# Zero stores in a later slot, one group of products behind a matmul group, other PSUM banks for two small tiles

## Chip, cores and metric

One core of a Trainium2 chip runs the whole kernel. The metric is the device time of one execution in microseconds (us); the kernel before has a median of 1085.94 us over three runs.

## The reference

Three stages follow each other. A linear attention runs over 768 tokens of 4 batches and 8 heads of 40 channels; per token the state decays by `w`, loses a rank-one correction, and gains one:

```python
for t in range(S):
    y[:, :, t] = einsum('bhd,bhde->bhe', r[t], state)
    Sa = einsum('bhde,bhe->bhd', state, a[t])
    state = state * w[t] - einsum('bhd,bhe->bhde', Sa, b[t])
    state = state + einsum('bhd,bhe->bhde', v[t], k[t])
```

Its output, as 3072 rows of 320, goes through a gated product `x = (x @ w_a * (x @ w_b)) @ w_out` with an inner width of 1536. Last comes a layer of 8 experts: each row goes to the expert with the largest gate logit, `max(x @ w1[e], 0) @ w2[e]` with an inner width of 1024, scaled by the gate weight.

## The kernel before

**Attention and up projection (`phase1`).** The 768 tokens are cut into 12 chunks of 64. The recurrence inside a chunk is solved as matmuls with a triangular inverse, so a chunk needs: its decay products (`gp`, from `w`), score matrices per batch, the inverse of a 64 x 64 triangle, and a forward pass that carries the state. The loop `for c in range(NCH + 1)` has 24 slots `i` per step, and the dictionary `STEADY` (line 378) says which piece runs in which slot. Pieces of several chunks stand in one step: the forward pass of chunk c, scores and inverse for c+1 and c+2, loads for c+3.

Four engines (TensorE, VectorE, ScalarE, GpSimd) run their instructions in the order in which the program is written (`manual_schedule`). SyncE, which issues most transfers, is not among them; its queue is ordered by the scheduler. An engine stops at an instruction whose data or buffer is not there, and all that is written behind it on that engine waits too.

What matters around the change, by slot:

- Slot 5, for 2 <= c < 10: one store of zeros `zt` to the DRAM buffer `xs` (line 351), eight stores of 805 KB each. A memset of `zt` on GpSimd (line 498) stands two slots earlier. Expert rows are scattered into `xs` much later.
- Slot 5: `relayout` (line 690) reads the decay products out of the buffer of `w` into `gp`. Slot 7: `load_w` (line 534) loads `w` of a later chunk, 366 KB, into the one buffer `w`. Slots 11, 12, 13 and 15: `spans` (line 557), four checks of the range of `w` on ScalarE; their result is used only at the end of the kernel.
- Slots 7 and 19: `uv` loads (line 798). Slots 9 and 20: `vn` loads on ScalarE's queue (line 792). Slots 10 and 1: `r`. Slot 15 and 0: `bk` (line 540). Slots 18 and 20: `at` (line 589).
- Slots 7, 8, 15, 19: scores (lines 631 to 641); one slot after a pair is done its part `nd` is sent to DRAM (line 648), and `tinv` (lines 700 to 745) loads it back as `m` and a unit matrix as `xt`, builds the inverse of 32 x 32 blocks on VectorE (lines 716 and 722, two instructions for each of 31 rows) and sends it through DRAM into `s`.
- `t21a` (line 747) in slot 22 for batch pair 0 and in slot 26, which is slot 2 of the next step, for pair 1: two transposes on VectorE (line 755, `t`), 32 products of 32 x 32 on TensorE (line 759, `ta`, two PSUM banks) and two evictions on ScalarE (line 766, `pt`). `t21b` (lines 778 and 782, `tb`) follows two slots later and completes the triangle. The forward pass `forward` (lines 827 to 850, `px` and `pu`, evicted into `vn` and `xs`) stands in every second slot.
- Odd slots from 3 on: two up-projection groups from the list `units` (lines 338 to 341). A group is eight matmuls into one PSUM bank (line 1115, `pm`), evicted on ScalarE for `w_a` (line 1118, `ua`) and multiplied on VectorE for `w_b` (line 1127, `uh`), and stored every second time (line 1129, `hT`).

PSUM is cut in two pools: five banks under the tag `pa` (`psA`) for attention, down products and the like, three under `pm` (`psM`) for the groups.

**Down projection and gate (`MoeDown.run`).** It multiplies `hT` by `w_out` (line 1268, `py`), computes gate and expert number, counts slots (line 1303, `pr`, a tile of `psM`) and scatters each row to `xs` by indirect DMA on GpSimd (line 1321).

**Experts (`Experts.run`).** A list of jobs: (0, 0, 256) is the first 256 rows of expert 0, (0, 256, 384) the next 384, then the other experts. A job gathers its rows from `xs` (line 1515, `x`), transposes them on TensorE (line 1540), runs `up` (line 1562, `u`, eight tiles in `psM`, each read by ScalarE at line 1564 as `hh` and by VectorE at line 1565 as `hl`) and `down` (line 1582). The last counts and scatters of the gate stand inside job 0's `up`. In job 1's `up`, after the sixth tile, `said` (line 1607) adds up the verdict of all range checks: the product `pb` of the operand `bb` with ones, in `psM`.

Of the kernel before, what the change touches and what calls it, by code (L numbers as in the profile page):

```python
# [8 lines left out]
F32 = mybir.dt.float32  # L9
# [30 lines left out]
def kernel_body(tc, I, out, stage="full", dbg=None):  # L40
    nc = tc.nc
    ctx = ExitStack()
    with ctx:
# [36 lines left out]
        with ExitStack() as moe:  # L80
            with tc.manual_schedule(engines={E.PE, E.DVE, E.Activation, E.Pool}):
                down = None if stage == "up" else MoeDown(tc, I, moe, psA, psM, ident, hT, wo, xs)
                phase1(tc, I, cst, drm, psA, psM, ident, hT, mk_ident, wo, xs, span, tiny, down)
                if stage == "up":
                    return
                experts = Experts(tc, I, moe, psA, psM, ident, xs, out)
                down.run(experts, span, tiny, flag)
# [45 lines left out]
def phase1(tc, I, cst, drm, psA, psM, ident, hT, mk_ident, wo, xs, span, tiny, down):  # L133
    nc = tc.nc
# [3 lines left out]
    A = Attention(tc, I, att, mid, cst, drm, psA, ident, dv, ot, span)  # L138
# [46 lines left out]
    tinv = A.tinv(0)  # L185
# [16 lines left out]
    t1 = A.tinv(1, (uh, view(xt)))  # L202
# [8 lines left out]
    mix(t1[:lead], [lambda: A.forward((0, 0))] + conv.take(n3))  # L211
    t1 = t1[lead:]
    over = [A.spans(0, [t[:120, 0:L // 2].bitcast(F32) for t in sp])]
    units, tinv = [], t1
    for c in range(NCH + 1):
        T = dict(STEADY)
        if c == 0:
# [8 lines left out]
        for i in range(24):  # L226
# [41 lines left out]
                    A.t21b(c1, pr)  # L268
            if 1 <= c < NCH:
                for pr in on("t21a", i + 24):  # L270
                    A.t21a(c, pr)
                for pr in on("t21b", i + 24):
                    A.t21b(c, pr)
            for m in range(3):
# [63 lines left out]
            if i % 2 and (i >= T["group"] or len(units) > 24):  # L338
                for g in units[:2]:
                    g()  # L340
                units = units[2:]
            more = []
            if c < 2:
# [14 lines left out]
            n = T["tinv"][i]  # L358
            mix(tinv[:n], dv.take() + more)
            tinv = tinv[n:]  # L360
            if i == T["inverse"] and c2 < NCH:
                assert not tinv
                tinv = A.tinv(c2)
# [22 lines left out]

    "t21a": [22, 26], "t21b": [24, 28],
    "tinv": [0, 0, 2, 3, 5, 5, 2, 2, 5, 5, 5, 5, 5, 5, 5, 5, 3, 0, 0, 0, 0, 0, 0, 0],
    "group": 2, "fill": 5, "dsg": 2, "dxf": 0, "dtake": 3, "dh": 1, "dst": 3,
}  # L390
LAST = {"open": 21, "free": 6, "w": [1, 11], "load": [18, 20, 22], "gate": 14, "conv": [21, 22]}

# [72 lines left out]
def urow(b, o):  # L465
    return slice(C * (b % 2) + o, C * (b % 2) + o + R)


class Attention:
# [274 lines left out]
            out.append(lambda s=s, box=box: sub(s, box))  # L744
        return out

    def t21a(self, c, pr):

        nc = self.nc
        st = self.st[c]  # L750
        bs = 2 * pr, 2 * pr + 1
        s1 = [st["s1"][pr][:, x] for x in range(2)]
        t11 = self.p2.tile([128, 8, R], F32, tag="t11", name=f"t11_{c}_{pr}", bufs=1)
        for b in bs:
            nc.vector.transpose(out=t11[urow(b, 0)], in_=s1[b % 2][urow(b, 0), :, 0:R])  # L755
        pa = [self.ps.tile([128, 512], F32, tag="pa", name=f"ta{c}_{b}") for b in bs]
        for h in range(H):
            for b in bs:
                nc.tensor.matmul(  # L759
                    pa[b % 2][urow(b, R), R * h:R * h + R], s1[b % 2][urow(b, 0), h, R:C], t11[urow(b, 0), h, :],  # L760
                    start=True, stop=True)
        p = self.p2.tile([128, 8, R], F32, tag="pt", name=f"pt{c}_{pr}", bufs=1)
        st["p", pr] = p
        for b in bs:
            q = urow(b, R)
            nc.scalar.mul(p[q], pa[b % 2][q, :8 * R].rearrange("p (h t) -> p h t", t=R), -1.0)
# [653 lines left out]
class Experts:  # L1420
# [128 lines left out]
    def up(self, j, n, xt, then):  # L1549
        nc, p2 = self.nc, self.p2  # L1550
        x, ids, xh, xl = xt
        h1, l1 = self.w1[JOBS[j][0]]
        hs = []
        for f in range(FF2 // 128):
            fs = slice(128 * f, 128 * f + 128)
            p = self.psM.tile([128, 512], F32, tag="pm", name=f"u{j}_{f}")[:, 0:n]
            seq = [(h1[:, k, fs], xl[:, k]) for k in range(2)]
            seq += [(l1[:, k, fs], xh[:, k]) for k in range(2)]
            seq += [(h1[:, 2, fs], xl[:, 2]), (h1[:, 2, fs], xh[:, 2])]
            seq += [(h1[:, k, fs], xh[:, k]) for k in range(2)]  # L1560
            for i, (l, r) in enumerate(seq):
                nc.tensor.matmul(p, l, r, start=(i == 0), stop=(i == len(seq) - 1))
            hh, hl = (p2.tile([128, 512], F32R, tag=t, name=f"{t}{j}_{f}", bufs=12)[:, 0:n] for t in ("hh", "hl"))
            nc.scalar.activation(out=hh, in_=p, func=AF.Relu)  # L1564
            nc.vector.scalar_tensor_tensor(  # L1565
                out=hl, in0=p, scalar=0.0, in1=hh.bitcast(F32), op0=ALU.max, op1=ALU.subtract)
            hs.append((hh, hl))
            for g in then.get(f, ()):
                g()
        return hs  # L1570
# [21 lines left out]
    def verdict(self, ones, span, tiny, over, flag):  # L1592

        nc, p1 = self.nc, self.pw
        bb = p1.tile([128, 6], BF16, name="bb", bufs=1)
        nc.vector.memset(bb, 0.0)
        sp = p1.tile([120, 4], F32, name="sp", bufs=1)
        nc.vector.tensor_reduce(out=sp, in_=span, op=ALU.add, axis=AX.X)
        nc.vector.tensor_scalar(bb[0:120, 0:4], sp, 0.0, 0.0, op0=ALU.is_le, op1=ALU.is_equal)
        nc.vector.tensor_copy(bb[:, 4:5], over)  # L1600
        cn = p1.tile([128, 1], F32, name="cn", bufs=1)
        nc.vector.tensor_reduce(out=cn, in_=tiny[:, 0:NTINY], op=ALU.add, axis=AX.X)
        nc.vector.tensor_scalar(bb[:, 5:6], cn, 0.0, 0.0, op0=ALU.is_le, op1=ALU.is_equal)

        def said():
            pb = self.psM.tile([128, 6], F32, tag="pm", name="pb")
            nc.tensor.matmul(pb, ones, bb, start=True, stop=True)
            nc.vector.tensor_reduce(out=cn, in_=pb, op=ALU.max, axis=AX.X)
            nc.vector.tensor_scalar(flag, cn, 0.0, None, op0=ALU.is_gt)

        self.said = said

    def run(self, hooks):
        self.p2 = self.ctx.enter_context(self.tc.tile_pool(name="e2", bufs=2))
        s1 = lambda e: [lambda k=k: self.split1(e, k) for k in range(3)] if e < NE else []
        s2 = lambda e: [lambda k=k: self.split2(e, k) for k in range(4)] if e < NE else []
        for j, (e, off, n) in enumerate(JOBS):
            up, down = {}, {}
            put = lambda d, at, f: d.setdefault(at, []).append(f)
            if j == 0:  # L1620
                for at, f in hooks.items():
                    put(up, at, f)
            elif j == 1:
                put(up, 2, self.late)
                put(up, 5, lambda: self.said())
                for k, f in enumerate(s1(1) + [lambda: self.load1(2)] + s2(1) + [lambda: self.load2(2)]):
                    put(up, min(1 + k, 7), f)
                for k, f in enumerate(s1(2)):
                    put(down, min(k, 2), f)
            else:  # L1630
                for k, f in enumerate(s2(e + 1)):
                    put(up, 2 + k, f)
                for k, f in enumerate(s1(e + 2)):
                    put(down, min(k, 2), f)
# [265 lines left out]
```

## Time and profile before

| | us |
|---|---|
| runs | 1087.28, 1081.84, 1085.94 |
| median | 1085.94 |
| the profiled execution | 1086.37 |
| its span in the trace | 1084.6 |
| busy in it: TensorE matmul | 961.4 |
| VectorE | 705.0 |
| ScalarE | 572.8 |
| GpSimd | 391.6 |

The span runs from the first to the last instruction of the profiled execution. Names in rows are `out<-in` by the program's tile names; L759 is line 759 of the kernel before. PE is TensorE's matmul, DVE VectorE, ACT ScalarE, POOL GpSimd, SPq the queue of SyncE. A bracket at the end of a timeline row gives the idle time of the engine ahead of the row and what ended it. PEclk is TensorE's granted clock as a share of full speed.

### The profile page before, as it was taken

How to read it: one execution, taken by the hardware profiler on the slowest of the kernel's cores; microseconds unless marked ns; L12 is line 12 of the kernel's file. 1: busy time of each engine (PE TensorE's matmuls, PEld its weight loads, DVE VectorE, ACT ScalarE, POOL GpSimd, SP SyncE). 2: the span in 40 equal slices, each digit the busy share in tenths (PEclk: the TensorE clock that was granted, in tenths of full speed). 3: DMA queues.
4: the chain of work that ended last, by engine and by line, in shares of the span. 5: the costliest groups of instructions: out<-in, count | busy, mean ns of one | idle time of the engine just before them, and what ended most of it. 6: DMA issues, size and time to landing. Idle time of an engine off the chain costs nothing. (4 is left out here: it accounts for less than half of the span.)

```text
span 1084.6 us, 28183 instructions
## 1 busy us (share of the span) xinstructions
PE 961.4 (89%) x10879; PEld 909.3 (84%) x10879; DVE 705.0 (65%) x1891; ACT 572.8 (53%) x1365; POOL 391.6 (36%) x433
## 2 busy tenths in 40 slices
PE   4145389899999999999999999999999999999994
PEld 3045378899999899999999999899999889999994
DVE  8699589797978879797986832356568542222330
ACT  5357777666666566666665443433344354444530
POOL 4326544424232323234232112002226277666641
PEclk9655669999999999999999999999999999999998
DMA  8563454677686858678684233665665454444500
GB/s 206 143 179 82 113 132 106 158 142 172 162 191 165 178 153 165 156 157 173 154 197 119 60 91 108 186 187 162 184 200 173 160 168 146 133 150 144 160 16 17
DMA packets 218667, 158.59 MB, mean 146 GB/s; under 512 B 125269, under 2 KB 200630, under 8 KB 218524
## 3 DMA queue, kind: packets, MB, share of 16 engines
q1 hardware_dynamic: 205196, 137.33, 50.5%
q0 software_dynamic: 9808, 15.76, 4.8%
q10 hardware_dynamic: 3520, 3.61, 1.2%
q8 instruction: 88, 1.44, 0.6%
q14 instruction: 55, 0.45, 0.1%
HBM read 108.08 MB, written 44.60 MB: 141 GB/s over the span
## 5 line engine op out<-in xcount | busy, mean ns | idle before, releaser
L716 DVE TENSOR_TENSOR tmp<-m,xt 128x126 f32<-128x126 f32 (+22 forms) x372 | 117.6, 316 | 50.9 <-DMA xt<-in_one 34.9
L1115 PE MATMUL pm<-xl,wh 128*128 128x256 f32 x576 | 131.1, 310 | 4.8 <-ACT ua L1118 3.6
L1565 DVE SCALAR_TENSOR_TENSOR hl<-u,hh 128x384 fp32r<-128x384 f32 (+5 forms) x72 | 41.5, 580 | 142.4 <-ACT hh L1564 142.4
L722 DVE TENSOR_TENSOR xt<-xt,tmp 128x126 f32<-128x126 f32 (+22 forms) x372 | 115.5, 310 | 9.1
L1115 PE MATMUL pm<-xh,wl 128*128 128x256 f32 x576 | 116.7, 284 | 0.0
L1115 PE MATMUL pm<-xh,wh 128*128 128x256 f32 x576 | 116.2, 284 | 0.0
L1115 PEld LDWEIGHTS pm<-xl,wh 128*128 128x128 f32 x576 | 89.0, 193 | 11.4 <-ACT ua L1118 4.9
L1127 DVE TENSOR_TENSOR uh<-pm,ua 128x256 f32<-128x256 f32 x144 | 59.7, 416 | 57.3 <-PE pm L1115 43.0
L1268 PE MATMUL py<-wl,hh 128*128 128x328 f32 x288 | 91.1, 316 | 0.0
L1268 PE MATMUL py<-wh,hl 128*128 128x328 f32 x288 | 90.3, 313 | 0.8 <-DVE hl L1258 0.8
L1115 PEld LDWEIGHTS pm<-xh,wh 128*128 128x128 f32 x576 | 90.6, 193 | 0.0
L1115 PEld LDWEIGHTS pm<-xh,wl 128*128 128x128 f32 x576 | 90.4, 193 | 0.0
L1268 PE MATMUL py<-wh,hh 128*128 128x328 f32 x288 | 90.2, 313 | 0.0
L919 POOL TENSOR_SCALAR_AFFINE_SELECT s<-s 64x512 f32<-64x512 f32 x56 | 43.6, 778 | 117.7 <-ACT s L917 115.3
L1115 PE MATMUL pm<-xh,w 128*128 128x256 f32 x288 | 82.1, 285 | 0.0
L1115 PE MATMUL pm<-xl,w 128*128 128x256 f32 x288 | 82.0, 285 | 0.0
L1582 PE MATMUL dn<-l,hh 128*128 128x320 f32 (+3 forms) x240 | 75.0, 313 | 0.0
L1582 PE MATMUL dn<-h,hl 128*128 128x320 f32 (+3 forms) x240 | 74.1, 309 | 0.0
L1582 PE MATMUL dn<-h,hh 128*128 128x320 f32 (+3 forms) x240 | 74.1, 309 | 0.0
L1321 POOL DMA_INDIRECT xs<-xr,si x24 | 28.6, 1192 | 125.5 <-DVE acc L1316 74.5
L1118 ACT COPY ua<-pm 128x256 f32<-128x256 f32 x144 | 53.3, 370 | 38.1 <-PE pm L1115 37.0
L759 PE MATMUL ta<-t,s 32*32 32x32 f32 x768 | 22.8, 200 | 56.4 <-DVE t L755 52.4
(276 smaller groups left out, 2745.6 us busy)
## 6 DMA issues: line engine op xcount, KB each, us to landing
hT<-uh SPq DMA_DIRECT2D x72, 256.0 KB, 3.2
hf<-hT SPq DMA_DIRECT2D x36, 512.0 KB, 3.7
r<-in_moe_w SPq DMA_DIRECT2D x8, 1280.0 KB, 5.8
r<-in_moe_w SPq DMA_DIRECT2D x8, 1024.0 KB, 6.7
bk<-in_bk SPq DMA_DIRECT2D x22, 360.0 KB, 4.6
xs<-zt SPq DMA_DIRECT2D x8, 805.0 KB, 10.4
m<-nd SPq DMA_DIRECT2D x44, 128.0 KB, 3.6
at<-in_a SPq DMA_DIRECT2D x24, 180.0 KB, 4.5
```

Of the source, the lines that this page charges most:

```text
L716: nc.vector.tensor_tensor(box[0], m[2 * s // R][:, s % (R // 2):s % (R // 2) + 1, s + 1:].to_broadcast([128, rows, n]), xt[:, :rows, s:s + ...
L722: nc.vector.tensor_tensor(xt[:, :rows, s + 1:], xt[:, :rows, s + 1:], box[0], op=ALU.subtract)
L759: nc.tensor.matmul(pa[b % 2][urow(b, R), R * h:R * h + R], s1[b % 2][urow(b, 0), h, R:C], t11[urow(b, 0), h, :], start=True, stop=True)
L919: nc.gpsimd.affine_select(out=s2t[q * C:q * C + C], in_=s2t[q * C:q * C + C], pattern=[[0, 8], [1, C]], base=0, channel_multiplier=-1, com ...
L1115: nc.tensor.matmul(p, l, r, start=(i == 0), stop=(i == len(seq) - 1))
L1118: nc.scalar.copy(a, p)
L1127: nc.vector.tensor_tensor(h[:, f % 2], p, a, op=ALU.mult)
L1268: self.nc.tensor.matmul(py, self.pair[i][l][:, k, s], self.W[r][:, first + k, cols], start=(first + k == 0 and n == 0), stop=(first + k == ...
L1321: self.nc.gpsimd.indirect_dma_start(self.xs[:], bass.IndirectOffsetOnAxis(ap=si[:, i:i + 1], axis=0), xr[:, j, :], None, bounds_check=NE * ...
L1565: nc.vector.scalar_tensor_tensor(out=hl, in0=p, scalar=0.0, in1=hh.bitcast(F32), op0=ALU.max, op1=ALU.subtract)
L1582: nc.tensor.matmul(p, l[:, q], r[:, f], start=(f == 0 and i == 0), stop=(f == len(hs) - 1 and i == 2))
```

## The change

The zeros go from slot 5 to slot 9 (their memset from slot 3 to slot 7). `t21a` is cut in two: `turned` makes the two transposes, `t21a` the products and evictions. For pair 1 of chunks 1 to 11 the transposes stay where they were, and the rest runs after the first of the two `pm` groups of slot 3. Pair 0 keeps its order. In the experts the odd `u` tiles of job 0 and the tile `pb` are taken from `psA`.

```diff
-    units, tinv = [], t1
+    units, tinv, products = [], t1, []
...
             if 1 <= c < NCH:
                 for pr in on("t21a", i + 24):
-                    A.t21a(c, pr)
+                    A.turned(c, pr)
+                    products.append((c, pr))
...
                 for g in units[:2]:
                     g()
+                    if products:
+                        A.t21a(*products.pop())
                 units = units[2:]
...
-    "group": 2, "fill": 5, "dsg": 2, "dxf": 0, "dtake": 3, "dh": 1, "dst": 3,
+    "group": 2, "fill": 9, "dsg": 2, "dxf": 0, "dtake": 3, "dh": 1, "dst": 3,
...
-    def t21a(self, c, pr):
+    def turned(self, c, pr):
...
         for b in bs:
             nc.vector.transpose(out=t11[urow(b, 0)], in_=s1[b % 2][urow(b, 0), :, 0:R])
+        st["t11", pr] = t11
+
+    def t21a(self, c, pr):
+
+        nc = self.nc
+        st = self.st[c]
+        if ("t11", pr) not in st:
+            self.turned(c, pr)
+        t11 = st["t11", pr]
+        bs = 2 * pr, 2 * pr + 1
+        s1 = [st["s1"][pr][:, x] for x in range(2)]
         pa = [self.ps.tile([128, 512], F32, tag="pa", name=f"ta{c}_{b}") for b in bs]
...
-            p = self.psM.tile([128, 512], F32, tag="pm", name=f"u{j}_{f}")[:, 0:n]
+            pool, tag = (self.psA, "pa") if j == 0 and f % 2 else (self.psM, "pm")
+            p = pool.tile([128, 512], F32, tag=tag, name=f"u{j}_{f}")[:, 0:n]
...
-            pb = self.psM.tile([128, 6], F32, tag="pm", name="pb")
+            pb = self.psA.tile([128, 6], F32, tag="pa", name="pb")
```

## Rows read from the trace of the kernel before

**Rows 1.** The page: TensorE's busy tenths in 40 slices of 27 us.
```profile
PE   4145389899999999999999999999999999999994
```

**Rows 2.** Stretches: us, busy time of PE, PEld, DVE, ACT, POOL, PEclk, DMA share, GB/s.
```profile
144.80:152.88 8.08, 4.74 (x60) 4.32 (x57) 6.04 (x16) 5.54 (x14) 4.68 (x6) 0.54 0.72 185
...
294.47:342.33 47.86, 47.48 (x707) 44.84 (x704) 41.44 (x114) 31.16 (x80) 14.30 (x21) 1.00 0.78 172
342.33:394.39 52.06, 49.34 (x709) 46.28 (x705) 41.50 (x115) 31.18 (x80) 15.13 (x22) 0.97 0.74 158
...
443.27:491.37 48.10, 47.50 (x708) 44.84 (x705) 40.80 (x113) 32.26 (x84) 13.98 (x20) 1.00 0.76 169
...
245.73:540.09 294.36, 287.38 (x4229) 270.69 (x4225) 247.45 (x678) 186.44 (x479) 87.19 (x120) 0.99 0.76 166
```

**Rows 3.** Waits by engine: who waits <- for whom: us in total, times, longest.
```profile
ACT junk L557 <- DMA w<-in_w: 14.8, 6, 4.3
...
SPq L648 <- DMA xs<-zt: 33.6, 7, 5.6
...
DVE tmp L716 <- DMA xt<-in_one: 34.9, 7, 6.5
...
PE ta L759 <- ACT vn L846: 3.4, 10, 0.3
```

**Rows 4.** DMA issues: transfer, queue, count, KB each, us from issue to landing.
```profile
bk<-in_bk SPq DMA_DIRECT2D x22, 360.0 KB, 4.6
xs<-zt SPq DMA_DIRECT2D x8, 805.0 KB, 10.4
...
w<-in_w SPq DMA_DIRECT2D x11, 366.1 KB, 8.3
```

**Rows 5.** Timeline of SyncE and TensorE, one step: start, us, engine, line, instruction.
```profile
359.97 0.56 SPq L351 DMA_DIRECT2D xs<-zt  x1
...
363.24 0.46 SPq L534 DMA_DIRECT2D w<-in_w  x1
...
374.29 0.80 PE L1115 MATMUL pm<-xl,wh 128*128 128x256 f32 x2 [2.13 <-ACT ua L1118]
```

**Rows 6.** Timeline around pair 1's `ta` at 302, and pair 0's at 245.
```profile
302.44 0.24 PE L759 MATMUL ta<-t,s 32*32 32x32 f32 x2
303.03 0.69 PE L759 MATMUL ta<-t,s 32*32 32x32 f32 x30 [0.34 <-ACT vn L846]
303.65 0.51 PE L1115 MATMUL pm<-xl,wh 128*128 128x256 f32 x2
...
304.71 0.40 PE L1115 MATMUL pm<-xl,wh 128*128 128x256 f32 x2
...
307.52 0.69 PE L778 MATMUL tb<-s,pt 32*32 32x32 f32 x32
...
304.34 0.78 ACT L766 ACTIVATE pt<-ta 32x256 f32<-32x256 f32 x2
...
245.73 0.69 PE L759 MATMUL ta<-t,s 32*32 32x32 f32 x32
246.35 0.50 PE L1115 MATMUL pm<-xl,wh 128*128 128x256 f32 x2
```

**Rows 7.** Timeline of TensorE and VectorE around chunk 1's pair 1.
```profile
148.25 0.28 PE L759 MATMUL ta<-t,s 32*32 32x32 f32 x2 [3.15 <-DVE t L755]
...
153.06 0.42 DVE L1127 TENSOR_TENSOR uh<-pm,ua 128x256 f32<-128x256 f32 x1 [2.03 <-PE pm L1115]
```

**Rows 8.** Timeline of TensorE and VectorE in the first two expert jobs.
```profile
846.61 0.17 PE L1303 MATMUL pr<-oh,tri 128*128 128x8 bf16 x1 [1.42 <-DVE hl L1565]
...
857.62 0.27 PE L1540 MATMUL xt_0l<-ident,x 64*128 64x64 f32 x1 [0.49 <-DMA x<-xs]
...
872.69 0.17 PE L1607 MATMUL pb<-bb,ones 128*128 128x6 bf16 x1 [1.85 <-DVE hl L1565]
...
872.02 0.16 DVE L1603 TENSOR_SCALAR bb<-cn 128x1 bf16<-128x1 f32 x1
```

## The prediction

> **What bounds the kernel now.** I read the busy slices of the page first: from the sixth slice (136 us) TensorE is busy eight tenths, and from the ninth nine tenths or more, up to the last [rows 1]. So a gain after the start must come out of TensorE's few idle spots or out of work it does at half clock. The table by stretch comes second. I cut the loop at the first `ta` product of pair 0, once per chunk: one step is a row. A quiet step lasts 47.86 us with 47.48 of TensorE in it; the step from 342.33 lasts 52.06, and the granted clock falls to 0.97 there [rows 2]. Third come the waits by engine: ScalarE waits 14.8 us in 6 places for the load of `w`, and SyncE's queue 33.6 us in 7 places for the zeros to land [rows 3]. The DMA issues say why: 805 KB of zeros take 10.4 us to land and `w`, issued behind them, takes 8.3, where `bk`, a load of the same size, takes 4.6 [rows 4]. The timeline then follows the worst step: zeros issued at 359.97, `w` at 363.24, and at 374.29 TensorE waits 2.13 us for a `ua` that ScalarE evicts late, because the range check of `w` (`spans`, line 557) stood before it in ScalarE's order and waited 4.3 us [rows 3, 5].
>
> A second engine is nearly as late. VectorE waits 34.9 us in 7 places, 5 us each, at the start of the triangular inverse (line 716) for the `xt` that is loaded after the `nd` rows [rows 3]; then it works through to the transpose (line 755) that pair 0's `ta` waits for. In the quiet step from 294.47 it has 41.44 us of work [rows 2]; with that 5 us wait it fills 46.4 of the 47.86. What TensorE gains in a step is therefore only partly kept: the chain `nd` sent, `nd` back, inverse, transpose, `ta` gives a pace of its own.
>
> **Part 1, zeros from slot 9.** Eight stores (chunks 2 to 9) go from slot 5 to slot 9 and their memset from slot 3 to 7 on GpSimd, which has 14.30 us of work in a 47.86 us step [rows 2]; that move costs nothing. What the store passes on SyncE's queue: `rawo`, the two `uv` loads and, the point of it, `w` (slot 7). `w` then leaves before the zeros. At the pace of `bk` it lands in 4.6 us and not 8.3 [rows 4], 3.7 sooner; the mean wait is 14.8/6 = 2.5 us [rows 3], the longest 4.3, so five of the six should vanish and the longest shrink to about 0.6. Behind the zeros now come `r` (slot 10), `hT`, `bk` (15), `at` (18, 20) and the second `nd` send. `r` is first used in slot 19, `bk` and `at` in the next step; slots are 47.86/24 = 2.0 us, so each has 16 us or more against the 10.4 us of the zeros. The closest is `vn` (slot 9, ScalarE's queue, used in slot 14): 10 us. I charge nothing for these and keep a late `vn` in the range.
>
> What it is worth: the six steps from 245.73 to 540.09 take 294.36 us [rows 2]. Afterwards I take each at 48.0, the mean of the two steps among them that show no such stall, 47.86 and 48.10 [rows 2]: these are what TensorE and the VectorE chain do together, so 6 × 48.0 = 288.0 and the gain is 6.4 us, part 2's share in these steps included (the chain swallows it). Bounds: if only the 52.06 step is mended and the others stay at their mean, (294.36 − 52.06)/5 = 48.46, the gain is 294.36 − 6 × 48.46 = 3.6. If TensorE alone sets the pace, 47.48 less the 0.41 of part 2 is 47.07, and the gain 11.9. I take 6.4, nearest to measured steps.
>
> **Part 2, pair 1's `ta` behind the first group of slot 3.** The transposes stay in slot 2; the 32 small products and two evictions `pt` move behind one group of eight `pm` matmuls. Today `ta` starts at 302.44, stops after two products for a PSUM bank that ScalarE's `vn` eviction frees (0.34 us), and the next work starts at 303.65: 1.21 us [rows 6]. Pair 0's `ta`, without such a wait, takes 246.35 − 245.73 = 0.62 [rows 6]. The wait occurs 10 times [rows 3]. The `pm` group needs a bank of the other PSUM pool and runs 304.71 − 303.65 = 1.06 us [rows 6]; put first, it outlasts the bank wait (to 303.03), so `ta` runs undisturbed: 1.21 − 0.62 = 0.59 saved. Splitting the two groups adds one change of work; I charge 0.18, an estimate: a first `pm` takes 0.51 behind other work and 0.40 behind the pair's other group [rows 6], 0.11 more, and the way back somewhat less. Net 0.41 per step. Cover for the later `pt`: `ta` now ends near 304.3 instead of 303.65, `pt` runs 0.78 us on ScalarE, and `tb`, which needs it, starts at 307.52 [rows 6]: over 2 us are left for the evictions that now stand ahead of it. If they do not fit, `tb` waits what is missing, less than 1 us. Of the ten steps the six above are counted; the other four (chunks 2, 9, 10, 11) give 4 × 0.41 = 1.6, at worst 0.
>
> Chunk 1 is a case by itself. There `ta` waits 3.15 us for the transpose, at 148.25, and VectorE in turn waits 2.03 us for the `pm` group queued behind that `ta` [rows 7]. With the group first, TensorE works in that hole. VectorE is what paces this stretch: it can get back at most its 2.03; the group runs at the lower of the two clocks (granted 0.54 in this stretch [rows 2]), so its 1.06 become about 2 of the 3.15 us, and `ta` itself cannot move. I take 1.3, between 0 and 3.15.
>
> **Part 3, other banks in the experts.** Half of the first job's `u` tiles and the verdict's `pb` go from the three-bank pool to the five-bank one. At 846.61 the product `pr` waits 1.42 us for a bank that a `u` of job 0 holds until VectorE's `hl` [rows 8]. That wait goes, but at 857.62 TensorE waits 0.49 us for gathered rows `x` that hang on the scatter of `xs`, not on TensorE [rows 8]: what is won before is waited for there. I count 0, between −1 and 1.4. `pb` waits 1.85 us at 872.69 for such a bank; its operand `bb` is there from 872.02 + 0.16 = 872.18 [rows 8]. So it can start 0.5 sooner and no more: 0.5, between 0 and 0.5.
>
> **Sum.** 6.4 + 1.6 + 1.3 + 0 + 0.5 = 9.8 us. The profiled execution took 1086.37 (span 1084.6), the median of the three runs is 1085.94, 0.4 below. 1086.4 − 9.8 = 1076.6.
>
> **Rivals.**
> *A: the stalls move instead of going.* The 805 KB still cross the same DMA engines in the same step; if `w` still comes late, or the next loads behind the zeros do, or the inverse waits as much longer as TensorE comes sooner, term 1 is lost and 1.6 + 1.3 + 0.5 = 3.4 remain: 1083.0. For it: the 33.6 us that `nd` waits behind the zeros [rows 3] show that what is queued within 10 us of them is held, and VectorE's slack is under 2 us a step. Against: users of what comes behind have 16 us. The Trainium skill, "DMA: Bandwidth & Descriptors", section "Issuing engines are not separate DMA queues", says that queues of different engines run on the same 16 DMA engines and interleave; by that rule `vn`, from ScalarE's queue, shares them with the zeros from now on. No row shows the two together in one slot. Chance 0.22.
>
> *B: slower, SyncE still issues the zeros first.* Only four engines have a written order; SyncE's queue is ordered by the scheduler, and `w` must wait until the `gp` relayout has read its buffer. If the zeros, ready when their memset is done, leave just ahead of the later `w`, the 363.24 − 359.97 = 3.3 us that `w` now has between them [rows 5] shrink to nothing. ScalarE's wait then grows by 3.3 us in seven steps, and the 52.06 − 48.0 = 4.1 us that a 4.3 us wait cost [rows 2, 3] says that TensorE pays nearly all: 7 × 3.3 = 23 less the 3.4 of the other parts, 1106; if half is covered, 1094. I put it at 1100. It decides at the issue order alone: `w` must leave before the zeros. Against: today the order on SyncE is the program's at this place. Chance 0.11.
>
> *C: TensorE alone sets the pace.* The inverse's loads come sooner with the zeros away from them, and all is kept: 11.9 + 1.6 + 1.3 + 0.5 = 15.3, so 1071.1. Against: VectorE's 41.44 us of work and 5 us wait per step. Chance 0.07.
>
> **How the numbers follow.** The forecast, 1076.6, has the remaining 0.60; with the bounds of its terms it lies between 1072 and 1080.5. About 0.5% (5.4 us) is what a measurement of this kernel can tell from no change. Faster by more means below 1080.5: forecast and C, 0.67. Within: A, 0.22. Slower: B, 0.11. The range from 1071 to 1085 holds the forecast, A and most of C and leaves out B.
>
> **What would show it.** Right: `w` issued ahead of the zeros on SyncE and landing in 5 us; ScalarE's wait at line 557 under 4 us in total; the step from 342.33 near 48; `pm` between transpose and `ta` in every step from chunk 1; no wait of `ta` for `vn`. Wrong: steps of 48.5 or more without a stall of `ua`, with TensorE waiting at pair 0's `ta` for the transpose (A); waits of `px` for `vn`; zeros ahead of `w` (B); steps of 47.1 (C). The forecast fails if the VectorE chain has less slack than the two quiet steps show.

## The result and the profile after

| | before | after |
|---|---|---|
| median of 7 runs each, us | 1085.94 | 1078.53 |
| lowest and highest | 1078.62 to 1091.08 | 1074.71 to 1079.83 |
| profiled execution (span) | 1086.37 (1084.6) | 1079.83 (1078.1) |

The ratio is 0.992 with a 95% interval of 0.9892 to 0.9949: faster by 7.4 us by the medians, where the forecast was 9.8 from one profile to the other. The two profiles are 6.5 apart. The ratios here and below are those on record with their intervals; they are not exactly the quotients of the medians (0.9932 here).

The stretches of the changed kernel, cut as in [rows 2] (us, busy PE, PEld, DVE, ACT, POOL, clock, DMA share, GB/s): a quiet step, the step that took 52.06 before, the longest step, and the six together.

```profile
292.70:340.33 47.63, 47.38 (x704) 44.72 (x705) 41.46 (x114) 31.22 (x80) 14.51 (x21) 1.00 0.80 175
340.33:388.40 48.07, 47.57 (x708) 44.83 (x705) 41.28 (x114) 31.12 (x80) 14.57 (x21) 1.00 0.76 168
484.04:532.31 48.27, 47.53 (x705) 44.76 (x705) 40.94 (x114) 30.81 (x79) 14.60 (x21) 1.00 0.74 166
244.54:532.31 287.77, 285.12 (x4229) 268.76 (x4225) 247.75 (x679) 186.72 (x479) 87.25 (x121) 1.00 0.76 170
```

Six steps of 288.0 were forecast, 287.77 were measured: 6.6 us less than the 294.36 of [rows 2]. The granted clock stays at 1.00.

SyncE's timeline shows the new order: `w` leaves 6.5 us ahead of the zeros (in [rows 5] it left 3.3 behind them).

```profile
358.89 0.34 SPq L537 DMA_DIRECT2D w<-in_w  x1
360.45 0.39 SPq L1143 DMA_DIRECT2D hT<-uh  x1
360.89 4.43 SPq L651 DMA_DIRECT2D nd<-s  x4
365.42 0.42 SPq L354 DMA_DIRECT2D xs<-zt  x1
```

ScalarE has no wait for `w` left from 150 to 645 us. TensorE's waits there:

```profile
PE ta L773 <- DVE t L758: 2.8, 10, 0.6
PE py L950 <- POOL s L933: 2.6, 4, 1.6
PE ta L773 <- ACT ua L1132: 0.5, 2, 0.3
...
PE pm L1129 <- ACT ua L1132: 0.2, 1, 0.2
PE pm L1129 <- DVE uh L1141: 0.2, 1, 0.2
```

The ten waits of `ta` for `vn` [rows 3] are gone, and `ta` now waits ten times for the transpose. Pair 1's `ta`, to be held against [rows 6], runs as one block between two groups, and `tb` follows with no gap:

```profile
302.00 0.69 PE L773 MATMUL ta<-t,s 32*32 32x32 f32 x32
302.63 0.50 PE L1129 MATMUL pm<-xl,wh 128*128 128x256 f32 x2
...
305.54 0.69 PE L792 MATMUL tb<-s,pt 32*32 32x32 f32 x32
```

302.63 − 302.00 = 0.63 us against the 1.21 of before. In chunk 1 a group now stands ahead of the wait, which is 2.04 us and no longer 3.15 [rows 7]:

```profile
146.31 0.63 PE L1129 MATMUL pm<-xh,wh 128*128 128x256 f32 x2
148.98 0.22 PE L773 MATMUL ta<-t,s 32*32 32x32 f32 x2 [2.04 <-DVE t L758]
```

And in the experts, against [rows 8], `pr` starts without a wait, `xt` waits longer, and `pb` waits for its operand `bb`, not for a bank:

```profile
839.88 0.17 PE L1317 MATMUL pr<-oh,tri 128*128 128x8 bf16 x1
...
851.51 0.27 PE L1554 MATMUL xt_0l<-ident,x 64*128 64x64 f32 x1 [2.85 <-DMA x<-xs]
...
865.94 0.18 PE L1622 MATMUL pb<-bb,ones 128*128 128x6 bf16 x1 [1.21 <-DVE bb L1618]
```

By these two profiles the first and largest term of the sum looks right to 0.2 us, 6.6 for 6.4. The experiments say that it was not right for the reason given.

### The profile page after: what moved, and what is told of

Its sections match the earlier page's. It is cut to its first block, busy times and chain, and to the rows that moved or that the text cites. A ratio compares the mean times of both kernels' runs of the same rounds, so it can differ in the third digit from the quotient of the medians.

```text
span 1078.1 us, 28172 instructions
## 1 busy us (share of the span) xinstructions
PE 960.7 (89%) x10879; PEld 908.2 (84%) x10879; DVE 697.2 (65%) x1891; ACT 573.2 (53%) x1365; POOL 392.5 (36%) x433
## 4 chain that ended last, share of the span: by engine, by line
PE 67%; DVE 10%; DMA 9%; issue 4%; ACT 4%; POOL 2%; SPq 2%; ACTq 0%; POOLq 0%; DVEq 0%
PE pm L1129 22%; PE py L1282 9%; PE u L1577 8%; PE dn L1597 8%; PE s1p L634 3%; PE p L921 3%; PE pp L905 2%; DVE tmp L719 2%; DVE xt L725 2%; PE py L950 2%; PE px L850 1%; PE ta L773 1%; DMA out<-y,ids 1%; PE tb L792 1%; PE px L841 1%
## 5 line engine op out<-in xcount | busy, mean ns | idle before, releaser
L719 DVE TENSOR_TENSOR tmp<-m,xt 128x126 f32<-128x126 f32 (+22 forms) x372 | 115.4, 310 | 50.0 <-DMA xt<-in_one 31.5
L933 POOL TENSOR_SCALAR_AFFINE_SELECT s<-s 64x512 f32<-64x512 f32 x56 | 43.4, 775 | 114.9 <-ACT s L931 112.4
L644 POOL TENSOR_SCALAR_AFFINE_SELECT s<-s 64x512 f32<-64x512 f32 x48 | 33.8, 704 | 98.3 <-ACT s L642 88.6
```

Of the source, the lines that this page charges most:

```text
L644: nc.gpsimd.affine_select(out=v, in_=v, pattern=[[0, 8], [1, C]], base=0, channel_multiplier=-1, compare_op=ALU.is_gt, fill=0.0)
L719: nc.vector.tensor_tensor(box[0], m[2 * s // R][:, s % (R // 2):s % (R // 2) + 1, s + 1:].to_broadcast([128, rows, n]), xt[:, :rows, s:s + ...
L933: nc.gpsimd.affine_select(out=s2t[q * C:q * C + C], in_=s2t[q * C:q * C + C], pattern=[[0, 8], [1, C]], base=0, channel_multiplier=-1, com ...
```

## Experiments

Each group of runs stands beside runs of the kernel before on its own chip, and these differ: a median of 1081.6 us beside the parts and the repeated whole, 1079.84 beside the places of the zeros and the whole without part 3, 1084.06 beside the rest.

### The parts, each alone

Part 1 alone (`"fill": 5` becomes 9, nothing else):

```diff
-    "group": 2, "fill": 5, "dsg": 2, "dxf": 0, "dtake": 3, "dh": 1, "dst": 3,
+    "group": 2, "fill": 9, "dsg": 2, "dxf": 0, "dtake": 3, "dh": 1, "dst": 3,
```

> Part 1 alone: zeros from slot 9, nothing else. My theory (w ahead of the zeros ends ScalarE's waits, and the steps then run at the pace that VectorE's chain and TensorE give together): the six steps between the first ta of pair 0 near 245 and the one near 540 fall from 294.4 us to between 287.5 and 289, each within 47.6 to 48.4, and the time falls by 5 to 6.5 us; ScalarE waits under 4 us at line 557. Rival (the gain of the change lies in the moved products, which remove a wait in every step): under 3 us, steps with a quiet range check unchanged.

Measured: 1079.19 us against 1081.6 of the kernel before beside it, ratio 0.9979 (0.9962 to 0.9996). The steps and the waits of ScalarE came out as my theory said (no wait for `w` at all), the time did not: 2.3 us, not 5 to 6.5. Its six steps:

```profile
245.43:534.32 288.89, 285.03 (x4228) 268.99 (x4225) 247.11 (x679) 186.99 (x480) 87.54 (x121) 1.00 0.72 170
```

Part 2 alone (the change without `"fill": 9` and without `psA` in the experts):

```diff
-                    A.t21a(c, pr)
+                    A.turned(c, pr)
+                    products.append((c, pr))
...
                     g()
+                    if products:
+                        A.t21a(*products.pop())
```

> Part 2 alone: pair 1's products behind the first group of slot 3. My theory: 0.4 us in each step that TensorE paces and little in those where it already waits at pair 0's ta for the transpose, so 1.5 to 3 us in all; the stall of ua near 374 stays, ScalarE still waits some 15 us for w. Rival (products carry the change): 5 us or more. Rival (splitting the pair of groups costs what the wait cost): 0.

Measured: 1076.25 against 1081.6, ratio 0.994 (0.9917 to 0.9962): 5.4 us, the rival's number and not mine. ScalarE still waits 12.1 us for `w` in 7 places, and TensorE 2.6 us behind it.

Part 3 alone:

```diff
-            p = self.psM.tile([128, 512], F32, tag="pm", name=f"u{j}_{f}")[:, 0:n]
+            pool, tag = (self.psA, "pa") if j == 0 and f % 2 else (self.psM, "pm")
+            p = pool.tile([128, 512], F32, tag=tag, name=f"u{j}_{f}")[:, 0:n]
...
-            pb = self.psM.tile([128, 6], F32, tag="pm", name="pb")
+            pb = self.psA.tile([128, 6], F32, tag="pa", name="pb")
```

> Part 3 alone: odd u tiles of job 0 and pb in the other PSUM pool. My theory: pr no longer waits 1.42 us for hl, but TensorE waits longer at the first transposes of job 1 for the gathered rows, so nothing is left there; 0.5 us from pb. Time falls by 0 to 1 us. Rival (TensorE paces the tail, its clock stays up): 1.9 us and more.

Measured: 1082.42 against 1081.6, ratio 0.9996 (0.9977 to 1.0015). No gain can be seen. TensorE's wait for `hl` at `pr` is gone, and it waits 3.1 us for the gathered rows at `xt`: the wait moved, as forecast. In the five profiles without part 3 that wait at `xt` is 1.5 us at most, in the nine with it 1.9 to 4.4.

The whole change once more, on the same chip:

> The whole change again, beside the parts on one chip, for the sum and for a second profile. My theory: parts 1 and 2 overlap, so the whole gains less than the sum of the parts by 1 to 2 us; 6 to 9 us below the kernel before. Open: in the first profile of the whole change 3.9 us were lost between 820 and 840 us, where ScalarE waited 3.8 us for a load of expert weights (1.6 before). If that belongs to the change it is here again; if it is chance of that execution the gain at 810 us is kept to the end.

Measured: 1077.15 against 1081.6, ratio 0.9956 (0.9938 to 0.9974), 4.5 us. The parts alone sum to 2.4 + 5.4 − 0.8 = 7.0 by the medians; the whole is no better than part 2 alone. The loss between 820 and 840 us is there again, 2.9 us of `py` waiting for `hl`. The 4.5 us stand nearer rival A's 3.4 than the 9.8 of the forecast.

### Was the 52 us step the kernel's or the execution's?

A second profile of the kernel before, unchanged:

> The kernel before once more, for a second profile of the same program. If the step of 52.06 us belongs to the kernel, it is there again and the six steps take about 294 us with some 15 us of waits for w. If it was a chance of that execution, no step exceeds 50 us, the six take 287 to 290 us, and the waits for w total 5 to 12 us, as in the two kernels that kept the zeros in slot 5.

One execution of 1081.9 us. Its steps, cut as before (the second is the one that answers to the 52.06, the last the six together):

```profile
340.06:389.08 49.02, 47.58 (x708) 44.74 (x704) 40.57 (x113) 31.20 (x80) 14.22 (x20) 1.00 0.72 165
436.94:484.63 47.69, 47.35 (x708) 44.79 (x704) 41.66 (x114) 31.88 (x83) 14.29 (x21) 1.00 0.74 171
244.43:532.23 287.80, 284.39 (x4228) 268.60 (x4224) 248.74 (x679) 187.35 (x480) 86.43 (x121) 1.00 0.74 170
```

The six steps take 287.80 us with the zeros ahead of `w`, the same as the changed kernel's 287.77. So 6.5 us of the 294.36 are not the kernel's everywhere: they belonged to that execution, or to its chip and session. The same program waits for `w` 14.8 us in one profile and 3.9 in the other. Its wait for `w`, and its waits on TensorE:

```profile
ACT junk L557 <- DMA w<-in_w: 3.9, 3, 3.0
...
PE ta L759 <- ACT vn L846: 3.4, 10, 0.3
...
PE pm L1115 <- ACT ua L1118: 0.7, 2, 0.5
PE pm L1115 <- DVE uh L1127: 0.6, 1, 0.6
```

What repeats exactly is the wait of part 2, 3.4 us in 10 places; what does not is the one of part 1: TensorE's waits at `pm` for `ua` and `uh` are 1.3 us here, 4.6 in the first profile.

### Where the zeros stand

In slot 6, and in slot 7 behind the load of `w` (there `"fill": 7`), both with the rest of the change:

```diff
-    "group": 2, "fill": 9, "dsg": 2, "dxf": 0, "dtake": 3, "dh": 1, "dst": 3,
+    "group": 2, "fill": 6, "dsg": 2, "dxf": 0, "dtake": 3, "dh": 1, "dst": 3,
```

> The whole change but with the zeros in slot 6, one slot ahead of the load of w. SyncE sends zeros, two uv loads, w. My theory, that the order of zeros and w is what matters: w leaves 1 to 2 us behind the zeros instead of 3.3, lands later than in the kernel before, ScalarE waits 15 to 35 us at line 557 and TensorE loses 4 to 20 us against the whole change. Rival, that the loads' exact place matters little since the stall near 374 in the first profile of before was a rare one: within 2 us of the whole change.

> The whole change but with the zeros in slot 7, directly behind the load of w. If order alone decides: no wait of ScalarE for w above 1 us, time within 1.5 us of the whole change. If the zeros must be clear of w by some microseconds, w lands at 7 us or later and ScalarE waits 8 us or more in total.

Measured: 1074.24 and 1074.5 against 1079.84, ratios 0.9955 (0.9935 to 0.9976) and 0.9943 (0.9922 to 0.9964). In slot 6 the queue still sent zeros, `rawo`, two `uv`, `w`, with 3.2 to 3.8 us from zeros to `w`: the order of the kernel before, so the closer spacing was not tried. ScalarE waited 5.5 us in 5 places; TensorE's six steps took 286.02 us, and the time is that of the other order. In slot 7 `w` leaves 0.4 us ahead of the zeros, and no wait for it is left; six steps, 285.80 us. The rows, slot 6 first:

```profile
244.75:530.77 286.02, 284.78 (x4229) 268.51 (x4226) 247.62 (x678) 187.41 (x480) 86.85 (x120) 1.00 0.74 171
```

```profile
243.75:529.55 285.80, 284.77 (x4229) 268.70 (x4225) 247.39 (x678) 186.66 (x480) 86.80 (x120) 1.00 0.71 171
```

The rival wins: with the rest of the change in place, which of the two goes first moved the time by less than these runs can tell. The same holds of the `nd` sends, which stood behind the zeros too: SyncE's wait for the zeros there [rows 3] is 27.1 us in slot 6 and gone in the profile after.

### A late `w` on purpose

```diff
-    "load_w": 7, "span": [11, 12, 13, 15], ...
+    "load_w": 9, "span": [11, 12, 13, 15], ...
```

> The whole change, but w loaded in slot 9 and not 7, 4 us later, still ahead of the zeros; the range check stays in slot 11. Measures what a late w costs TensorE. By the step of the prediction that priced it (a wait of 4.3 us cost a step 4.1) ScalarE waits 3 to 5 us in eight or nine steps, 30 to 40 us in total, and the kernel is 25 to 35 us slower than the whole change. If waits of ScalarE are mostly covered by evictions that have room, TensorE loses under a third of it: under 10 us.

Measured: 1079.36 against 1084.06, ratio 0.9964 (0.9935 to 0.9992). My step's 25 to 35 us are far off. First, `w` was late only once: ahead of the zeros it lands so soon that 4 us less room are enough. In the step from 391 us (SyncE and ScalarE) it is used, without a wait, 4.6 us after its issue:

```profile
413.00 0.40 SPq L537 DMA_DIRECT2D w<-in_w  x1
...
417.55 0.63 ACT L560 ACTIVATE junk<-w,wlim 120x384 bf16<-120x384 f32 x1
```

Over the seven steps with zeros the check began 4.5 to 5.4 us after the issue, against 7.8 to 10.0 in the first profile of before, where it waited in six of the seven. Second, the one wait, 3.27 us, cost its step, chunk 2's, 49.28 − 47.63 = 1.65 us, half of it (the six later steps take 287.81 us and have no wait for `w`). The wait on ScalarE and TensorE's share stand in the last rows:

```profile
197.64:246.92 49.28, 47.63 (x704) 44.75 (x704) 39.52 (x110) 31.30 (x80) 11.74 (x17) 1.00 0.70 157
295.67:343.30 47.63, 47.38 (x704) 44.71 (x704) 41.88 (x114) 31.18 (x80) 15.12 (x21) 1.00 0.77 175
```

```profile
227.23 0.61 ACT L560 ACTIVATE junk<-w,wlim 120x384 bf16<-120x384 f32 x1 [3.27 <-DMA w<-in_w]
...
228.25 0.50 PE L1129 MATMUL pm<-xl,wh 128*128 128x256 f32 x2 [1.40 <-ACT ua L1132]
```

### The whole change without part 3

The edit is the reverse of part 3 alone.

> Parts 1 and 2 without part 3. In the three profiles with part 3 the stretch from the middle of the down projection to job 1's transposes takes 61 to 62.6 us, in the three without it 56.9 to 59.1, and TensorE waits 2.3 to 3.1 us for the gathered rows x against 0.2 to 0.7. If part 3 causes that, this kernel is 2 to 4 us below the whole change, near 1073 to 1075 beside a kernel before of 1081.6, and the stretch takes under 59.5 us. If these were chances of six executions it equals the whole change within 1 us.

Measured: 1074.69 against 1079.84, ratio 0.9955 (0.9937 to 0.9972), which is the whole change's 0.9956. The stretch took 58.3 us. But in the kernel with zeros in slot 7, which has part 3, it took 59.1, in the one with slot 6 57.3, and in the second profile of before, without part 3, 62.6. So a stretch of 61 to 62.6 us comes with and without part 3; part 3 neither costs nor brings anything that can be seen in the time. Its six steps carry the answer on part 2, since it differs from part 1 alone by part 2 and nothing else:

```profile
244.03:530.41 286.38, 284.49 (x4228) 268.38 (x4225) 248.22 (x679) 186.98 (x480) 86.72 (x121) 1.00 0.73 171
```

288.89 − 286.38 = 2.5 us, 0.42 a step: in this pair of profiles, which come from two chips, part 2's 0.41 is kept whole in the steps where I had let the chain swallow it. Against the kernel before (287.80 in its second profile) it is 1.4 us.

### Taking VectorE's chain off TensorE

Pair 0's products behind a group too, and `xt` loaded ahead of `m`, alone and together:

```diff
                 for pr in on("t21a", i):
-                    A.t21a(c1, pr)
+                    if c:
+                        A.turned(c1, pr)
+                        products.append((c1, pr))
+                    else:
+                        A.t21a(c1, pr)
```

> The whole change, and pair 0's products too behind the first group of slot 23 (from chunk 2 on). In the profile of the whole change TensorE waits 0.2 to 0.7 us at pair 0's ta for the transpose in six steps, 2.8 us from 150 us on. If TensorE sets the pace and the transpose is only a little late, that wait goes and the steps come to 47.6: 1 us faster than the whole change, less what splitting the groups costs (0.18 a step by the prediction, 1.8 in all). If VectorE's chain sets the pace, the wait comes back elsewhere and nothing is won. Both say within 2 us of the whole change; the steps tell them apart, 47.6 to 47.8 in all of them against 47.6 to 48.3 as they are.

> The whole change, and the unit matrix xt loaded ahead of the four loads of m, not behind them. VectorE waits 31.5 us in 7 places for xt. Theory (the chain is a fraction of a us behind TensorE): the inverse starts 0.5 to 2 us sooner, all steps come to 47.6, waits of ta for the transpose fall under 1 us from 150 us on, and the time falls by 1 to 1.5 us. Rival (the chain sets the pace by much more): steps fall below 47.5 and the time by 3 us and more.

```diff
+        nc.sync.dma_start(xt, self.I["one"].rearrange("p (i t) -> p i t", t=R))
         for k in range(2):
             for q in range(2):
...
                     nc.sync.dma_start(t[p], st["nd"][k])
-        nc.sync.dma_start(xt, self.I["one"].rearrange("p (i t) -> p i t", t=R))
```

> Both of the last two at once. If TensorE alone is left as what sets the pace, this is no faster than xt_first and perhaps slower by the split, 0 to 2 us; the six steps take 285.8 us, TensorE's own pace, 47.63 each.

Measured against 1084.06: 1078.86 (0.9933, 0.9911 to 0.9956), 1079.92 (0.995, 0.9921 to 0.9978) and 1077.1 (0.9931, 0.9899 to 0.9962). None is clear of the whole change's 0.9956, so no version better than it is shown. With pair 0's products moved, TensorE has no wait for the transpose left, and the six steps are 285.91 us with 285.16 of TensorE in them, 1.9 under the first profile after and 1.0 under the second, but not under the 285.80 and 286.02 of the section on the zeros.

```profile
247.81:533.72 285.91, 285.16 (x4225) 268.44 (x4225) 249.62 (x679) 186.01 (x480) 87.27 (x120) 1.00 0.74 171
```

`xt` ahead of `m` failed: the six steps took 289.82 us. VectorE's wait did not shrink, it went to the other load, 42.6 us where both together had been 31.5 + 10.1 = 41.6 in the profile after:

```profile
DVE tmp L719 <- DMA m<-nd: 42.6, 9, 6.4
```

Together the two give 287.15 us for the six steps, not the 285.8 expected.

## Why the prediction was right, and where it was not

**Sign, size and range held.** 1076.6 was forecast and 1078.53 measured, inside the range, and by luck in part, as the terms show. Rivals A and C did not come true as a whole, and B's order (zeros ahead of `w`) did not come. A's number is not far off, though: in the later runs the whole change gained 4.5 us, and 5.2 without part 3, against A's 3.4. Its sum, term 1 lost and the small terms kept, is close to what the experiments leave, for another reason: the waits for `w` did go, but by the later runs they were not worth 6.4 us.

**The step that failed, by the later runs, is the sum's first term, 6.4 us.** I took the 294.36 us of one execution for the kernel's. Three profiles of programs whose first phase is the same, the kernel before twice and part 3 alone, give 294.36, 287.80 and 287.86; the first is the odd one. The 288.0 forecast for after was met, but the kernel before is there already in its other profiles. The term's price was too high as well: a wait of 4.3 us cost 4.1 in a step whose granted clock also fell to 0.97 [rows 2], the wait of 3.3 made on purpose cost 1.65 with the clock at 1.00. And the 8.3 us of `w` and the 10.4 of the zeros [rows 4] were no medians of many: the trace tells the landing of one of the eleven loads and of one of the eight stores. Part 1 alone shows 1.1 us more in the six steps than the ordinary 287.80, and with part 2 beside it 2.5 less (288.83 with part 2 alone, 286.38 with both). By the runs part 1 alone is worth 2.3 us, interval 0.4 to 4.1, and nothing on top of part 2 that the times show. What it does was foreseen correctly: `w` goes first and ScalarE does not wait for it.

One rival to this account is untested: that the chip or session of the first runs, and not that one execution, makes `w` late. No second profile of the kernel before was taken there. The profiled execution, 1086.37 us, was no slow one for its place (median 1085.94); the two profiles taken there have the highest DMA share of the six steps, 0.76 against 0.71 to 0.75; and the gain was 7.4 us there and 4.5 beside the parts. If so, the term was worth up to some 3 us more there than here, an estimate from these two gains.

**Part 2 was sized right per step.** The price is best seen where VectorE's chain has room, in the step from pair 1's `ta` of chunk 9 to that of chunk 10. The second profile of before and the profile after:

```profile
539.95:587.55 47.60, 47.26 (x711) 44.70 (x704) 35.96 (x104) 27.30 (x67) 12.40 (x16) 1.00 0.64 149
```

```profile
541.62:588.82 47.20, 47.20 (x706) 44.62 (x705) 35.84 (x103) 27.30 (x68) 12.60 (x17) 1.00 0.62 141
```

47.60 − 47.20 = 0.40, against 0.41 forecast; the 0.34 of idle time is gone. All four profiles without part 2 have 47.6 for this step, and the seven with it and with pair 0 and `xt` as they were 47.20 to 47.25. From pair 1's `ta` to the next work it is 1.2 us in each of the ten steps from chunk 2 on without part 2, and 0.62 in each with it. Pair 0's products behind a group as well make the same quiet step 47.39: 0.19 for the second split, forecast 0.18. Where I let the chain swallow the 0.41, in the six steps, it swallows about half: five profiles with part 2 and no large wait for `w` (all_again 286.95, after 287.77, without part 3 286.38, zeros in slot 6 286.02, in slot 7 285.80) have a mean of 286.6, the two ordinary ones without it 287.8. That is 1.2 us of 6 × 0.41 = 2.5, and the sum had none of it apart from term 1. The half is a rough figure: `w` in slot 9, with part 2 and no wait for `w` in these steps, took 287.81, and part 1 alone, without part 2, 288.89; with these two the means are 286.8 and 288.2.

Part of where it is swallowed can be seen at pair 0's `ta`, in the profile after:

```profile
340.33 0.24 PE L773 MATMUL ta<-t,s 32*32 32x32 f32 x2
340.79 0.66 PE L773 MATMUL ta<-t,s 32*32 32x32 f32 x30 [0.21 <-DVE t L758]
341.37 0.50 PE L1129 MATMUL pm<-xl,wh 128*128 128x256 f32 x2
```

341.37 − 340.33 = 1.04 us, where it was 0.62 without a stop [rows 6]: pair 0 stops for the transpose here, and the 0.42 that this costs is as much as part 2 had won at pair 1. Over the seven `ta` of pair 0 from chunk 3 to 9 such stops add up to 1.9 to 2.9 us in the seven profiles with part 2 and to 0.8 to 2.4 in the four without.

**Chunk 1's 1.3 us** came: from pair 0's `ta` of chunk 1 to that of chunk 2 the four profiles without part 2 took 61.8 to 63.2 us, mean 62.6, the five of the list above 61.2 to 61.5, mean 61.4. One more profile with part 2, that of `w` in slot 9, has 62.1, so the two ranges overlap a little.

**What the parts make together.** 1.2 in the six steps, 1.2 in chunk 1 and 1.2 in the four other steps (by the means of the same profiles 0.3 in chunk 2's, 0.5 in those of chunks 9 and 10, 0.4 from pair 0's `ta` of chunk 11 to the milestone named below) are 3.6 us for part 2. Alone it measured 5.4 by the medians, 4.1 to 9.0 by the interval of its ratio; the whole change beside it 2.8 to 6.7. So by the times it was not the range check and the zeros that carried the gain but the products, which I had given 2.9. Some 2 us of the 5.4 is traced to no place: in the profile of part 2 alone the six steps, with their waits for `w`, show none of the gain (288.83).

**The chain (rival A) is real, and part of its cost.** At the pace of the step with no wait the six would take 6 × 47.20 = 283.2 us after, an estimate; with part 2 and no large wait for `w` they took 285.8 to 287.8. TensorE waits 2.8 us at `ta` for the transpose in the profile after, 0.8 in the first of before. Part of that is TensorE being sooner at the same place. Part may be the zeros' new place: in part 1 alone, where TensorE's work is unchanged, `ta` waits 2.4 us for the transpose, and 0.2 in the second profile of before. One execution of each does not settle it.

**Part 3 was forecast at 0 for `u` and 0.5 for `pb`.** The first was right and for the reason given. For the second the wait for a bank became a wait for `bb` in the profile after; but the second profile of before and the one without part 3 have no wait at `pb` at all, so this too was a matter of the execution, and a gain of 0.5 is below what the runs show.

**What was left out of the sum:** the end of the down projection. From TensorE's milestone in the middle of it (the 200th product of one form of `py`) to the end of the span the kernels took 283 to 292 us, 286.0 and 288.3 in the two profiles that the forecast joins. There the changed kernel lost what part 1 seemed to win too much: `py` waits 3.1 us for `hl` where it waited 0.8. ScalarE, which has to make `hh` first, stands 3.8 us at a load of expert weights, against 1.6 in the first profile of before:

```profile
804.05 1.05 ACT L1483 CAST h<-r 128x1024 fp32r<-128x1024 f32 x1 [3.80 <-DMA r<-in_moe_w]
...
PE py L1282 <- DVE hl L1272: 3.1, 2, 2.3
PE xt_0l L1554 <- DMA x<-xs: 2.8, 1, 2.8
PE pr L1317 <- DVE oh L1302: 1.6, 1, 1.6
```

The second profile of the kernel before has 3.8 us at the same place, so it is not the change's:

```profile
PE py L1268 <- DVE hl L1258: 3.8, 3, 2.1
```

What makes that load late in some executions is left open. The two errors, a term from a profile with slow steps and an end that came out slow in the other, happened to meet near the right sum.

How much the change is worth stays uncertain by chip or session: 7.4 us by the first seven runs each, 4.5 beside the parts. The intervals of the two ratios share 0.9938 to 0.9949; a gain of 5.5 to 6.7 us would fit both.

## What to carry to other kernels

A wait that repeats at the same length at every step (0.34 us, ten times, in every profile with the products unmoved) is a safe term; a wait whose length differs from step to step in one profile (1.3 to 4.3 us) may be a matter of the execution or the chip, and before it carries a sum it wants a second profile or a price bounded by the quietest steps. Where two engines are nearly equal, price an edit both as kept and as swallowed and look which the quiet steps allow; here about half was kept where I had counted none, and part of the rest came back as a stop at the next place that hangs on the other engine. A transfer moved in a queue is judged by who is late afterwards: the loads of `xt` and `m` exchanged places and the sum of the wait stayed.

## What the runs showed of the hardware

A load of 366 KB issued ahead of the 805 KB store on the same queue was in use after 4.5 to 5.4 us (`w` in slot 9); behind it, after 7.8 to 10.0 in the one profile in which nearly every load was waited for, and after 6.6 to 8.3 for the three waited for in the second profile of before. The Trainium skill, "DMA: Bandwidth & Descriptors", section "Queues, rings and completion order", says that each DMA engine takes descriptors of one ring in order, and this agrees with it. Of the loads of `bk` that now stand behind the zeros the trace tells one landing in the six steps: 8.7 us in the profile after, where the same load took 4.9 in the profile before, and no engine waits for `bk`. By this one load the delay moved to what stands behind, and its users had the room that the prediction gave them.
